# Scaling the last two output tiles of a two-branch gated layer in halves, on ScalarE and VectorE

## The chip, the cores and the metric

The kernel runs on one core of a Trainium2 chip. The metric is device time in microseconds (us) of one execution; lower is better. The engines are TensorE (PE in the profile, with its weight loads as PEld), VectorE (DVE), ScalarE (ACT), GpSimd (POOL) and SyncE (SP); PSUM is the memory into which TensorE writes.

## The reference

Two branches work on the same input `x` of 2048 rows and 512 columns, and a gate of each row mixes them:

```
g = sigmoid((x * gate_w).sum(-1))
a = state-space branch: a complex linear recurrence over the 2048 rows, then
    2 * Re(h @ C^T) + x * Dskip
b = linear attention with 32 heads of 16 columns: features of q and k by softmax,
    num / (den + 1e-6), then @ wo
out = g * a + (1 - g) * b          (2048 x 512, bfloat16)
```

The input `B_x` is given but not used: both branches read `A_x`.

## The kernel before, in words

The 2048 rows are cut into 16 tiles of 128 rows. A tile of the output (a "row" in the rest of this text, numbered `n` from 0 to 15 in the order in which it is made) goes through three small generators, and each `yield` in them ends a step:

- `y{n}` (`st_y`, lines 709 to 723) begins the output of the row in a PSUM tile `py` of 128 partitions x 512 fp32 columns, which fills one PSUM bank. Its matmuls add the state-space branch (L717) and `x * Dskip` (L722).
- `o{n}` (`st_o`, lines 725 to 759) makes the attention branch of the row. Matmuls put the numerators and denominators into `pn` (L736); ScalarE takes the logarithm of the denominators, ScalarE or VectorE copies the numerators to `nu`, ScalarE makes `rd`, which holds the reciprocal denominators and also `(1 - g) / g`, and VectorE multiplies both into `on` (L744). For rows 12 to 15 (`OT_PE`) TensorE transposes `on` into a PSUM tile `po` (L753), and a copy brings it to `oT` in SBUF (`evac`, L119 on ScalarE or L121 on VectorE). For the other rows a transposing DMA does this (L758).
- `t{n}` (`st_t`, lines 761 to 774) ends the row. First step: four matmuls of `oT` with `Wo` add into `py` (L765). Second step: one instruction scales `py` by the gate of each row, `G[:, ti:ti + 1]`, and writes the bfloat16 tile `ot` (L769 on ScalarE, L771 on VectorE). Third step: one DMA of 128 KB writes `ot` to the output (L773).

No planner orders the work. A list written out by hand, `ORDER`, names the steps one by one, and the loop at the end of the kernel calls `next` on the named generator; every engine then executes its instructions in this order. A suffix `:D` on a step makes it use VectorE instead of ScalarE for its copy or scaling, `:A` sends its DMA from ScalarE's queue instead of SyncE's, and `@k` names the PSUM bank. The framework adds the waits between engines (semaphores) by itself, from the tiles that the instructions read and write. The list ends with:

```
... y13 t13 o14 o14@1 t15 t15 t15 o14:D t14 t13 t13 t14 t14:A
```

Read step by step: row 13's output matmuls; the product `on` of row 14; its transposes on TensorE; row 15's output matmuls, its scaling on ScalarE, its DMA from SyncE; the copy of row 14's `po` to `oT` on VectorE (`o14:D`); row 14's output matmuls; row 13's scaling and DMA; row 14's scaling on ScalarE and its DMA from ScalarE's queue. So row 15 ends before row 14, and row 14 is the last of all.

Of the kernel before, what the change touches and what calls it, by code (L numbers as in the profile page):

```python
# [10 lines left out]
ALU = mybir.AluOpType  # L11
# [57 lines left out]
def kernel(  # L69
# [18 lines left out]
    nc = tc.nc  # L88
    _, S, D = A_x.shape
# [5 lines left out]
    NTI = S // P  # L95
# [12 lines left out]
    VS = nc.vector.tensor_scalar  # L108
# [3 lines left out]
    sel = {"banks": [], "eng": "act"}  # L112
# [66 lines left out]
    G = const.tile([P, NTI], F32, name="G")  # L179
# [581 lines left out]
    def st_t(n):  # L761
        ti = order[n]
        py, oT = live["py", n], live["oT", n]
        for g in range(HG):
            MM(out=py[:], lhsT=oT[:, g, :], rhs=Wo[:, g, :], start=False, stop=(g == HG - 1))  # L765
        yield
        ot = pools["op"][1].tile([P, D], BF16, name="ot", bufs=14)
        if sel["eng"] == "act":
            nc.scalar.mul(out=ot[:], in_=py[:], mul=G[:, ti:ti + 1])  # L769
        else:  # L770
            VS(out=ot[:], in0=py[:], scalar1=G[:, ti:ti + 1], scalar2=None, op0=ALU.mult)  # L771
        yield
        sel["q"].dma_start(out=out_par[:, ti // 2, ti % 2, :], in_=ot[:])  # L773
        yield
# [17 lines left out]
    for n in range(NTI):  # L792
        st.update({f"k{n}": st_k(n), f"v{n}": st_v(n), f"q{n}": st_q(n), f"y{n}": st_y(n), f"o{n}": st_o(n), f"t{n}": st_t(n)})
# [10 lines left out]
    for tok in ORDER.split():  # L804
        tok, _, eng = tok.partition(":")
# [42 lines left out]
```

## Time and profile before

| | us |
|---|---|
| median of 3 timed runs | 155.96 (155.78 to 157.13) |
| time of the profiled execution | 155.28 |
| span of the profiled execution, first to last instruction | 153.2 |

| engine | busy us | share of the span |
|---|---|---|
| PE | 146.2 | 95% |
| DVE | 132.4 | 86% |
| ACT | 129.2 | 84% |
| POOL | 15.8 | 10% |

The profile is of one execution, and its time of 155.28 us lies 2.1 us above its span, which holds only what lies between the first and the last instruction. In a timeline row the columns are: start (us from the span's start), length (us), engine, source line, operation, output<-input, number of instructions merged into the row, and in brackets how long the engine had been idle and what ended it. A row with `q` behind the engine (`SPq`, `ACTq`) is of the engine's instruction sequencer, such as the issue of a DMA. In a group row the number before the bar is the count, then come the total busy time, the mean ns of one instruction, and the idle time ahead of them.

### The profile page before, as it was taken

The page shows a single profiled execution, that of the slowest core. Times are in us where ns is not written, and L with a number is a line of the kernel's source. Part 1 is how long each engine was busy: PE and PEld are TensorE (multiplying, and loading weights), DVE is VectorE, ACT ScalarE, POOL GpSimd, SP SyncE. Part 2 cuts the span into 40 slices and gives each one's busy share as a digit, 9 for nine tenths or more (in the row PEclk, how much of TensorE's full clock was granted, in tenths as well). Part 3 has the DMA queues.
Part 4 walks back from the last instruction along what each step waited for, and adds up shares of the span by engine and source line. Part 5 has one row for each costly group of instructions (what it writes and reads, how often), then busy time and mean ns, then how long its engine had stood idle before and what let it go on. Part 6 is the DMA issues. An engine that isn't in the chain of part 4 may idle for free.

```text
span 153.2 us, 3361 instructions
## 1 busy us (share of the span) xinstructions
PE 146.2 (95%) x1236; PEld 95.0 (62%) x1254; DVE 132.4 (86%) x303; ACT 129.2 (84%) x279; POOL 15.8 (10%) x43
## 2 busy tenths in 40 slices
PE   7899999999999999999999999999999999999990
PEld 7644434788878985869867656555554455555540
DVE  3799999999999999999999999999999958717520
ACT  3489998999998999999998999699498998627562
POOL 8239980000000000000000000000000000000000
PEclk9999999999999999999999999999999999999997
DMA  4875995534445699930000007711278859969842
GB/s 116 164 218 97 223 178 112 103 75 103 103 107 78 129 230 178 166 115 4 0 0 4 0 0 169 74 37 34 42 98 147 176 122 189 162 129 206 247 143 103
DMA packets 50848, 17.55 MB, mean 115 GB/s; under 512 B 44176, under 2 KB 50832, under 8 KB 50832
## 3 DMA queue, kind: packets, MB, share of 16 engines
q1 hardware_dynamic: 48976, 15.75, 53.8%
q10 hardware_dynamic: 1696, 1.57, 3.2%
q8 instruction: 10, 0.16, 0.5%
q0 software_dynamic: 160, 0.01, 0.2%
q14 instruction: 6, 0.05, 0.1%
HBM read 2.64 MB, written 2.10 MB: 31 GB/s over the span
## 4 chain that ended last, share of the span: by engine, by line
PE 78%; SPq 10%; DMA 7%; issue 1%; ACT 1%
PE pgq L601 18%; PE py L717 16%; PE pq L475 9%; PE py L765 8%; SPq L229 8%; PE pv L475 4%; PE ph L668 4%; PE pk L475 4%; DMA xT<-in_A_x_dram 4%; PE kvacc L578 3%; DMA phT<-EEq 3%; PE pn L736 3%; PE pgq L606 2%; PE py L722 2%; PE pgq L608 2%; SPq L284 1%
## 5 line engine op out<-in xcount | busy, mean ns | idle before, releaser
L601 PE MATMUL pgq<-xT,BT 128*128 128x256 bf16 x256 | 31.5, 272 | 0.0
L475 PEld LDWEIGHTS <-xT 128*128 128x128 bf16 x192 | 18.2, 98 | 18.3 <-DMA xT<-in_A_x_dram 0.7
L601 PEld LDWEIGHTS <-BT 128*128 128x128 bf16 x256 | 24.6, 98 | 4.1
L138 ACT ACTIVATE EEk<-EEk 128x1024 bf16<-128x1024 bf16 x20 | 20.4, 1080 | 0.0
L119 ACT CAST uv<-pgq 128x512 bf16<-128x512 f32 x28 | 15.9, 605 | 0.5 <-PE pgq L601 0.4
L475 PE MATMUL pv<-Wv,xT 128*128 128x512 bf16 x59 | 15.5, 379 | 0.3
L475 PE MATMUL pq<-Wq,xT 128*128 128x512 bf16 x60 | 15.4, 379 | 0.2
L765 PE MATMUL py<-Wo,oT 128*128 128x512 bf16 x62 | 15.3, 379 | 0.1
L475 PE MATMUL pk<-Wk,xT 128*128 128x512 bf16 x62 | 14.7, 379 | 0.3 <-DMA xT<-in_A_x_dram 0.2
L138 ACT ACTIVATE EEq<-EEq 128x1024 bf16<-128x1024 bf16 x12 | 11.7, 1042 | 0.3 <-DVE EEq L527 0.3
L769 ACT ACTIVATE ot<-py,G 128x512 bf16<-128x512 f32 x12 | 7.9, 686 | 4.5 <-PE py L765 4.3
L138 ACT ACTIVATE ld<-pn 128x16 f32<-128x16 f32 x32 | 6.1, 191 | 5.7 <-PE pn L736 4.6
L590 ACT ACTIVATE phT<-X,dgB 128x512 bf16<-128x512 bf16 x16 | 10.7, 725 | 0.0
L119 ACT CAST nu<-pn 128x256 bf16<-128x256 f32 x27 | 9.9, 380 | 0.0
L119 ACT CAST vx<-pv 128x512 bf16<-128x512 f32 x16 | 9.1, 604 | 0.4 <-PE pv L475 0.4
L548 DVE TENSOR_TENSOR EEk<-EEk,rck 128x4096 bf16<-128x4096 bf16 (+1 forms) x5 | 9.3, 1858 | 0.0
L744 DVE TENSOR_TENSOR on<-nu,rd 128x512 bf16<-128x512 bf16 x16 | 6.7, 421 | 2.8 <-ACT rd L138 1.6
L765 PEld LDWEIGHTS <-oT 128*128 128x128 bf16 x64 | 5.7, 97 | 5.3 <-DMA oT<-on 0.5
L119 ACT CAST Xq<-pq 128x512 bf16<-128x512 f32 x16 | 8.9, 608 | 0.0
L119 ACT CAST Xq<-pk 128x512 bf16<-128x512 f32 x15 | 8.6, 598 | 0.4 <-PE pk L475 0.4
L736 PEld LDWEIGHTS <-phT 128*128 128x128 bf16 x128 | 6.2, 97 | 3.8 <-DMA phT<-EEq 1.4
L511 DVE TENSOR_TENSOR smk<-smk 128x512 bf16<-128x512 bf16 (+4 forms) x18 | 8.1, 448 | 0.1
(178 smaller groups left out, 321.2 us busy)
## 6 DMA issues: line engine op xcount, KB each, us to landing
X<-HM SPq DMA_DIRECT2D x8, 256.0 KB, 4.5
out_dram<-ot ACTq DMA_DIRECT2D x8, 128.0 KB, 2.5
out_dram<-ot SPq DMA_DIRECT2D x8, 128.0 KB, 2.2
C2r<-in_B_wqkv_dram ACTq DMA_DIRECT2D x2, 256.0 KB, 3.8
Wv<-in_B_wqkv_dram SPq DMA_DIRECT2D x1, 512.0 KB, 4.0
Bn<-in_A_B_re_dram SPq DMA_DIRECT2D x1, 512.0 KB, 5.7
Bn<-in_A_B_im_dram SPq DMA_DIRECT2D x1, 512.0 KB, 6.8
Wo<-in_B_wo_dram SPq DMA_DIRECT2D x1, 512.0 KB, 4.3
```

The costliest lines, as they stand in the source:

```text
L119: nc.scalar.copy(out=out_ap, in_=in_ap)
L138: ins = nc.scalar.activation(**kw)
L229: nc.sync.dma_start_transpose(out=xT[:, :, ti * P:(ti + 1) * P], in_=x_res[ti // 2, ti % 2])
L475: MM(out=pt[:], lhsT=xT[:, kt, ti * P:(ti + 1) * P], rhs=W[:, kt, :], start=(kt == 0), stop=(kt == KT - 1))
L511: VT(out=dst, in0=cur[:, :, :, 0:n, :], in1=cur[:, :, :, n:2 * n, :], op=op)
L548: VT(out=E5, in0=E5, in1=rc.to_broadcast([P, L, 2 * NB, Dh, 4]), op=ALU.mult)
L590: nc.scalar.mul(out=t_, in_=x_, mul=c_)
L601: MM(out=pg[:, h, :], lhsT=BT[:, kt, 2 * j + h, :], rhs=xT[:, kt, r * NC:(r + 1) * NC], start=(h == 0 and kt == 0), stop=(r % 2 == 0 and k ...
L717: MM(out=py[:], lhsT=hs(r, t, slice(a * P, (a + 1) * P)), rhs=C2B[t], start=(t == 0), stop=False)
L736: MM(out=pn[:, 4 * m:4 * m + 4, :].rearrange("p h e -> p (h e)"), lhsT=ph[:, 4 * hf + m, :], rhs=KVm[:, 4 * hf + m, :], start=(m == 0), st ...
L765: MM(out=py[:], lhsT=oT[:, g, :], rhs=Wo[:, g, :], start=False, stop=(g == HG - 1))
L769: nc.scalar.mul(out=ot[:], in_=py[:], mul=G[:, ti:ti + 1])
```

## The change

For the last two rows, `n` of 14 and 15, the single scaling instruction becomes two. ScalarE scales columns 0 to 255 and VectorE columns 256 to 511 of the same `py` tile into the same `ot` tile. The suffix of the step is not looked at for these two rows. The list `ORDER` is the same word for word, the DMAs are the same, and rows 0 to 13 are scaled as before. The lines below the edit move down by three: L769 becomes L772, L771 becomes L774, L773 becomes L776; the new halves are L769 (ScalarE) and L770 (VectorE).

```
         yield
         ot = pools["op"][1].tile([P, D], BF16, name="ot", bufs=14)
-        if sel["eng"] == "act":
+        if n >= NTI - 2:
+            nc.scalar.mul(out=ot[:, 0:D // 2], in_=py[:, 0:D // 2], mul=G[:, ti:ti + 1])
+            VS(out=ot[:, D // 2:D], in0=py[:, D // 2:D], scalar1=G[:, ti:ti + 1], scalar2=None, op0=ALU.mult)
+        elif sel["eng"] == "act":
             nc.scalar.mul(out=ot[:], in_=py[:], mul=G[:, ti:ti + 1])
         else:
             VS(out=ot[:], in0=py[:], scalar1=G[:, ti:ti + 1], scalar2=None, op0=ALU.mult)
```

## The prediction, made before the changed kernel was run

> **What bounds the kernel now.** I read the head of the page first, then the chain that ended last at its tail, then the timeline of that tail.
>
> ```profile
> span 153.2 us, 3361 instructions
> PE 146.2 (95%) x1236; PEld 95.0 (62%) x1254; DVE 132.4 (86%) x303; ACT 129.2 (84%) x279; POOL 15.8 (10%) x43
> PE 78%; SPq 10%; DMA 7%; issue 1%; ACT 1%
> ```
>
> TensorE sets the pace of the whole kernel: it is busy 95% of the span and carries 78% of the chain. The change touches nothing but the last two rows of the output, so the shares of the whole run are no help. What counts is the last 6 us, where TensorE has run out of work. There the chain reads (start, length, what):
>
> ```profile
> 147.44 0.88 PE py L765 x4
> 148.32 0.02 issue
> 148.34 0.89 ACT ot L769 x2
> 149.23 0.27 issue
> 149.50 0.69 ACT ot L769
> ```
>
> After row 15's four output matmuls, ScalarE's three scalings stand in a row (t15, t13, t14) and the end hangs on the third. The timeline, asked in narrow windows so that merged rows come apart, shows the other engines around it:
>
> ```profile
> 147.28 0.38 PE L765 MATMUL py<-Wo,oT 128*128 128x512 bf16 x1
> 147.48 0.42 DVE L121 COPY oT<-po 128x512 bf16<-128x512 bf16 x1 [1.06 <-PE po L753]
> 147.96 0.10 PEld L765 LDWEIGHTS <-oT 128*128 128x128 bf16 x1
> 148.14 1.03 PE L765 MATMUL py<-Wo,oT 128*128 128x512 bf16 x4
> 148.34 0.69 ACT L769 ACTIVATE ot<-py,G 128x512 bf16<-128x512 f32 x1 [1.00 <-PE py L765]
> 148.93 1.25 ACT L769 ACTIVATE ot<-py,G 128x512 bf16<-128x512 f32 x2
> 149.50 0.69 ACT L769 ACTIVATE ot<-py,G 128x512 bf16<-128x512 f32 x1
> 150.22 0.34 ACTq L773 DMA_DIRECT2D out_dram<-ot  x1
> DMA to landing us min/median/max: 2.0/2.0/2.0
> ```
>
> The last row here is the landing time of that one final transfer. The reader is to see a piece of luck in the order: VectorE copies row 14's transposed tile (`oT<-po`) at 147.48, while TensorE is still on row 15's matmuls (first at 147.28). Row 14's weights are loaded at 147.96, and its four matmuls follow without a gap (148.14 to 149.17). ScalarE takes t15 at 148.34, t13 at 148.93 and t14 at 149.50, ends at 150.19, and the transfer goes out at 150.22. It lands 2.0 us later, at 152.2. The span ends about 1.0 us after that (153.2), with the closing waits of the program, and the profiled time of 155.28 us lies 2.1 us above the span.
>
> **The change part by part.** Two scalings of 128x512 on ScalarE become halves of 128x256, and VectorE gets two halves of 128x256. Nothing goes to another queue and no transfer is added. What decides is where the new instructions stand, and for what they wait. The built order of the changed kernel has at its end, engine by engine (line, instruction, tile, what it waits for):
>
> ```
> DVE  L770 ot_2496<-py_2290 128x256 [waits Activation]   row 15
>      L121 oT_2486<-po_2487 128x512                      row 14
>      L770 ot_2508<-py_2264 128x256 [waits Activation]   row 14
> ACT  L769 ot_2496<-py_2290 128x256 [waits PE]           row 15
>      L772 ot_2505<-py_2046 128x512                      row 13
>      L769 ot_2508<-py_2264 128x256 [waits PE]           row 14
>      L776 out<-ot_2508 [waits DVE]                      row 14
> SP   L776 out<-ot_2496 [waits DVE]                      row 15
> ```
>
> Two things follow. First, the halves do not run at once: each VectorE half waits for ScalarE's counter to count the ScalarE half of the same row, so a row's scaling takes the one half after the other. Second, the copy `oT<-po` of row 14 now stands on VectorE behind the row 15 half. It used to start at 147.48, and it must now wait for row 15's matmuls, for ScalarE's half and for VectorE's half. Behind that copy waits TensorE, with row 14's four matmuls, and behind those the end of the kernel.
>
> The prices of a half are not in the trace. The nearest groups are (mean ns of one after the bar):
>
> ```profile
> L769 ACT ACTIVATE ot<-py,G 128x512 bf16<-128x512 f32 x12 | 7.9, 686 | 4.5 <-PE py L765 4.3
> L119 ACT CAST uv<-pgq 128x512 bf16<-128x512 f32 x28 | 15.9, 605 | 0.5 <-PE pgq L601 0.4
> L119 ACT CAST nu<-pn 128x256 bf16<-128x256 f32 x27 | 9.9, 380 | 0.0
> L771 DVE TENSOR_SCALAR ot<-py,G 128x512 bf16<-128x512 f32 x4 | 3.0, 750 | 4.2 <-PE py L765 4.1
> L121 DVE CAST Wk<-pf 128x512 bf16<-128x512 f32 x2 | 1.4, 686 | 0.0
> L121 DVE CAST nu<-pn 128x256 bf16<-128x256 f32 x5 | 2.0, 423 | 2.6 <-ACT ld L138 2.6
> ```
>
> On ScalarE half the columns of a cast take 605 - 380 = 225 ns off; so a half scaling costs 686 - 225 = 461 ns, not 343. On VectorE they take off 686 - 423 = 263 ns; a half costs 750 - 263 = 487 ns, not 375. Bounds: halving the whole (343 and 375) from below, the whole itself (686 and 750) from above. I take the differences, since they come from the same engines on casts of these very sizes. So a row's two halves in turn cost about 0.46 + 0.49 = 0.95 us and a handover, where one scaling cost 0.69.
>
> The Trainium skill, "ScalarE: Activation LUTs", section "What ACT_TABLE_LOAD costs", gives an activation with a per-row operand as about 280 ns and 0.833 ns for each column: 707 ns for 512, where the trace has 686, and 493 ns for 256. With 493 ns for both ScalarE halves the sum below would be 0.06 us more.
>
> Handovers come from these rows:
>
> ```profile
> 140.03 0.18 ACT L138 ACTIVATE ld<-pn 128x16 f32<-128x16 f32 x1
> 140.25 0.42 DVE L121 CAST nu<-pn 128x256 bf16<-128x256 f32 x1 [0.26 <-ACT ld L138]
> 144.74 0.75 DVE L771 TENSOR_SCALAR ot<-py,G 128x512 bf16<-128x512 f32 x1
> 145.40 0.41 DVE L121 COPY oT<-po 128x512 bf16<-128x512 bf16 x1
> 22.88 0.11 PEld L475 LDWEIGHTS <-xT 128*128 128x128 bf16 x2 [0.65 <-DMA xT<-in_A_x_dram]
> 22.89 0.39 PE L475 MATMUL pk<-Wk,xT 128*128 128x512 bf16 x1 [0.16 <-DMA xT<-in_A_x_dram]
> ```
>
> ScalarE to VectorE takes 0.04 (140.21 to 140.25). A copy behind a scaling on VectorE starts 0.09 before the scaling's end (145.49, 145.40). VectorE's copy to the weight load takes 0.06 (147.90 to 147.96), and a waiting TensorE starts its first matmul 0.01 after the weight load (22.88, 22.89). The matmuls' end to ScalarE takes 0.03 (148.31, which is 147.28 and 1.03, to 148.34), and the last scaling's end to the issue of its transfer 0.03 (150.19 to 150.22).
>
> The sum, from 148.34, which the change leaves where it is:
> - row 15 on ScalarE 148.34 to 148.80; on VectorE 148.84 to 149.33
> - copy of row 14's tile 149.24 to 149.66 (0.42), where it ran 147.48 to 147.90
> - weight load 149.72, matmuls 149.73 to 150.76 (1.03), where they ended at 149.17
> - row 14 on ScalarE 150.79 to 151.25; on VectorE 151.29 to 151.78
> - transfer issued at 151.81 instead of 150.22: **+1.59 us**
>
> What lies beside this: row 13's scaling, on ScalarE from about 148.70 (0.10 ahead of the end before it, as at 148.93 against 149.03) to 149.38, is hidden in the wait for VectorE, so the 0.23 us gained there is lost. Row 15's transfer starts some 0.3 us later than before and row 13's behind it on SP's queue, both more than 1.5 us ahead of the last one, so they cost nothing; if that cover were gone, they would land at about 152, still ahead of 153.8. The last transfer still takes 2.0 us.
>
> So the profiled execution goes from 155.28 to 156.87 us. The three timed runs have a median of 155.96 (155.78 to 157.13), 0.68 above it; the forecast is the median and the difference, **157.55 us**.
>
> **The rivals.** (a) The halves do run at once, as the change's words have it, with the copy still behind the row 15 half. VectorE's half then runs 148.34 to 148.83, the copy 148.74 to 149.16, matmuls 149.23 to 150.26, both last halves until 150.78, issue 150.81: +0.59, 156.55 us. For it speaks that the trace shows ScalarE and VectorE busy together all along; against it stands the wait in the built order. The Trainium skill, "PSUM — Partial Sum Buffer", section "PSUM bank collisions raise a hardware error", says that software must keep two engines off the same bank and quadrant of partitions at any one time, for two reads as well. No run here shows what happens otherwise. By it the two halves of one row, which lie in one bank, could not be read together at all.
>
> (b) Not slower: the copy of row 14 gets through before row 15's half, because its input has been ready since about 147.46. Row 14's matmuls then end at 149.17 as before, ScalarE has its half at 149.28 to 149.74, VectorE its own until 150.27, issue 150.30: +0.08; with the halves at once, issue 149.77: -0.45, 155.51 us. It decides whether the copy starts before 148.34. Against it: VectorE's order puts the copy after the half, and rows 144.74 and 145.40 show a scaling and such a copy run one behind the other, in order.
>
> (c) TensorE now stands idle for 1.42 us (148.31 to 149.73), and if its clock were halved by then, the last four matmuls would take 2.06 instead of 1.03: +2.62, 158.58 us. What the trace has on it are windows after TensorE's last matmul (the granted clock is the number after the last bracket):
>
> ```profile
> 151.00:151.50 0.50, 0.00 (x0) 0.00 (x0) 0.00 (x0) 0.00 (x0) 0.00 (x0) 1.00 0.73 258
> 151.50:152.00 0.50, 0.00 (x0) 0.00 (x0) 0.00 (x0) 0.00 (x0) 0.00 (x0) 0.67 0.02 4
> 152.00:152.50 0.50, 0.00 (x0) 0.00 (x0) 0.00 (x0) 0.00 (x0) 0.00 (x0) 0.50 0.00 0
> ```
>
> The clock is still full at 151.50 and halves within the next slice, more than 2.3 us after the end at 149.17. An idle stretch of 1.42 us is shorter, so this is unlikely.
>
> **How the numbers follow.** My forecast, halves in turn with the copy behind them, has 0.84; (a) 0.07, (b) 0.04, (c) 0.05. A difference of 1% is 1.56 us, about what a measurement of this kernel can tell from no change, and my sum of 1.59 lies just above it. With halves at their lower bounds the sum would be 1.59 - 2 x (0.118 + 0.112) = 1.13, and at the upper ones 1.59 + 2 x (0.225 + 0.263) = 2.57. The handovers are taken at the tightest rows there are, so they lean upward. Of the 0.84 I put 0.55 over 1% and 0.29 within. Slower by over 1%: 0.55 and (c), 0.60. Within 1%: 0.29, (a) and half of (b), 0.38. Faster by over 1%: 0.02, the other half of (b), were more gained than its price. The forecast's own range is 157.1 to 158.5, by its bounds; the range given reaches down to (a), 156.5, and up to 158.5.
>
> **What would show it.** In the changed kernel's timeline: VectorE's first half starts right after ScalarE's half has ended, not with it; the copy `oT<-po` starts near 149.2; TensorE has a gap of about 1.4 us ahead of its last four matmuls, which still take 1.03; the last transfer is issued near 151.8; halves take about 0.46 and 0.49. It would be wrong if both halves started together, if TensorE had no gap there, or if the tail stood as before and the time differed elsewhere.

## The result, and the profile after

Over 18 runs each, the changed kernel takes 157.32 us (156.38 to 157.99) and the kernel before 155.49 us (154.82 to 157.23); the 18 of before include the three runs of the table above. The ratio is 1.0105, with a 95% interval of 1.0082 to 1.0129: the change makes the kernel 1% slower. The forecast was 157.55 us, 1.0102 times the median of before, in a range of 156.5 to 158.5. Executions come in a faster and a slower state, and all ratios and medians here are of the fast ones.

The head of the page of the changed kernel hides all this. TensorE's busy share is what it was, and the one trace of the change in the chain is that VectorE now has 1% of it (TensorE's 75% of the chain against 78% is none: a second profile of the kernel before has 82%):

```profile
span 155.7 us, 3362 instructions
PE 147.3 (95%) x1236; PEld 96.1 (62%) x1254; DVE 133.2 (86%) x305; ACT 128.9 (83%) x279; POOL 15.8 (10%) x43
PE 75%; SPq 10%; DMA 10%; issue 1%; DVE 1%; ACT 1%
```

The end of that chain (start, length, what) has become longer:

```profile
149.37 0.02 issue
149.39 0.48 ACT ot L769
149.87 0.02 issue
149.90 0.48 DVE ot L770
150.38 0.34 DVE oT L121
150.72 0.05 issue
150.77 1.05 PE py L765 x4
151.82 0.02 issue
151.84 0.48 ACT ot L769
152.32 0.02 issue
152.35 0.48 DVE ot L770
```

Before, this chain went through three scalings on ScalarE and was done. Now it goes from ScalarE's half of row 15 to VectorE's half, from there to the copy of row 14's tile (`oT`, L121), to row 14's four matmuls, and once more through a ScalarE half and a VectorE half. The timeline of the changed kernel shows the same from the engines' side, with the waits in brackets:

```profile
149.39 0.47 ACT L769 ACTIVATE ot<-py,G 128x256 bf16<-128x256 f32 x1 [0.87 <-PE py L765]
149.76 0.68 ACT L772 ACTIVATE ot<-py,G 128x512 bf16<-128x512 f32 x1
149.90 0.48 DVE L770 TENSOR_SCALAR ot<-py,G 128x256 bf16<-128x256 f32 x1 [1.98 <-ACT ot L769]
150.30 0.41 DVE L121 COPY oT<-po 128x512 bf16<-128x512 bf16 x1
150.77 1.04 PE L765 MATMUL py<-Wo,oT 128*128 128x512 bf16 x4 [1.42 <-DVE oT L121]
151.84 0.47 ACT L769 ACTIVATE ot<-py,G 128x256 bf16<-128x256 f32 x1 [1.40 <-PE py L765]
152.35 0.48 DVE L770 TENSOR_SCALAR ot<-py,G 128x256 bf16<-128x256 f32 x1 [1.64 <-ACT ot L769]
152.87 0.34 ACTq L776 DMA_DIRECT2D out_dram<-ot  x1
DMA to landing us min/median/max: 1.9/1.9/1.9
```

VectorE's half waits for `ACT ot L769`, the other half of its own row, and TensorE waits 1.42 us for `DVE oT L121`, a copy whose input was long ready. I call the stretch from the start of row 15's scaling to the issue of the last transfer the tail (in the profile of before it is 1.88 us; the expectations below have 1.87). It is 149.39 to 152.87 here, 3.48 us, against 148.34 to 150.22, 1.88 us, before: **+1.60 us**. (In these two profiles row 15's scaling also starts 1.05 us later, 149.39 against 148.34. What that is worth is a question for the experiments.)

### The profile page after: what moved, and what is told of

Same layout as the page of the kernel before. It is cut to its first block, busy times and chain, and to the rows that moved or that the text cites. A ratio compares the mean times of both kernels' runs of the same rounds, so it can differ in the third digit from the quotient of the medians.

```text
span 155.7 us, 3362 instructions
## 1 busy us (share of the span) xinstructions
PE 147.3 (95%) x1236; PEld 96.1 (62%) x1254; DVE 133.2 (86%) x305; ACT 128.9 (83%) x279; POOL 15.8 (10%) x43
## 4 chain that ended last, share of the span: by engine, by line
PE 75%; SPq 10%; DMA 10%; issue 1%; DVE 1%; ACT 1%
PE pgq L601 18%; PE py L717 14%; PE pq L475 9%; PE py L765 8%; SPq L229 8%; PE pv L475 4%; PE ph L668 4%; PE pk L475 4%; DMA xT<-in_A_x_dram 4%; DMA oT<-on 3%; DMA phT<-EEq 3%; PE kvacc L578 3%; PE pn L736 2%; PE pgq L606 2%; PE py L722 2%; PE pgq L608 2%
## 5 line engine op out<-in xcount | busy, mean ns | idle before, releaser
L772 ACT ACTIVATE ot<-py,G 128x512 bf16<-128x512 f32 x10 | 6.8, 688 | 4.1 <-PE py L765 4.0
```

## The experiments

Theory A puts the loss down to the copy of row 14 that stands behind row 15's VectorE half; rival B to the halves that run in turn; rival C to a delay ahead of the tail.

**Copy first.** The halves stay, and the copy goes ahead of row 15's scaling:

```
 ORDER (on top of the changed kernel)
-o14@1 t15 t15 t15 o14:D t14 t13 t13 t14 t14:A
+o14@1 t15 o14:D t15 t15 t14 t13 t13 t14 t14:A
```

> Both rows in halves as in the changed kernel, but the copy of row 14's transposed tile stands ahead of row 15's scaling in the step list. The tail is counted from the start of row 15's scaling to the issue of the last transfer: 1.87 us in the kernel before, 3.48 in the changed one. Theory A (the loss is the copy that stands behind row 15's VectorE half): row 14's matmuls end as before, ScalarE has row 14's half from about 0.96 to 1.43 and VectorE its own from 1.47 to 1.95, tail 1.98, time +0.1 us, ratio 1.001 to the kernel before. Rival B (the loss is the halves that run one after the other, each row paying it): two rows at 0.3 us each, +0.6, ratio 1.004. Rival C (the change delays the work ahead of the tail: row 15's scaling started 1.05 us later in the profile after): that delay stays, tail near 2.0 but time +1.1, ratio 1.007.

Measured: a ratio of 1.0006 (0.9973 to 1.0039), a tail of 1.96 us. VectorE's timeline of this kernel, with ScalarE's two halves and the last transfer:

```profile
148.72 0.42 DVE L121 COPY oT<-po 128x512 bf16<-128x512 bf16 x1 [1.27 <-PE po L753]
149.59 0.47 ACT L769 ACTIVATE ot<-py,G 128x256 bf16<-128x256 f32 x1 [1.00 <-PE py L765]
150.09 0.48 DVE L770 TENSOR_SCALAR ot<-py,G 128x256 bf16<-128x256 f32 x1 [0.95 <-ACT ot L769]
150.53 0.47 ACT L769 ACTIVATE ot<-py,G 128x256 bf16<-128x256 f32 x1
151.03 0.48 DVE L770 TENSOR_SCALAR ot<-py,G 128x256 bf16<-128x256 f32 x1 [0.46 <-ACT ot L769]
151.55 0.34 ACTq L776 DMA_DIRECT2D out_dram<-ot  x1
```

The copy waits only for its own transposes. Both rows still run their halves in turn, and all but 0.08 us of the loss is gone. The halves in turn are not free even so: row 14's half starts 0.94 us into the tail, where its whole scaling started at 1.16 before, since ScalarE has only half of row 15 ahead of it, and that nearly pays for VectorE's half behind it. Rival B falls by the tail, where two rows at 0.3 us would have made about 2.5 us; by the time it would not, since 0.6 us is a ratio of 1.0038, still inside the interval. Rival C wanted 1.007, which lies outside.

**Row 15 alone, row 14 alone.** The condition `n >= NTI - 2` becomes `n == NTI - 1` in the one and `n == NTI - 2` in the other.

> Halves for row 15 alone, row 14 whole on ScalarE. Theory A: the copy still stands behind row 15's VectorE half, so only row 14's halves are saved: tail 3.48 - (0.47 + 0.03 + 0.48) + 0.69 = 3.18, +1.30 us, ratio 1.008. Rival B: row 15's halves cost 0.3 and the rest comes from elsewhere: tail 2.2, +0.3, ratio 1.002. Rival C: tail 3.18 and 1.0 more ahead of it, +2.3, ratio 1.015.

> Halves for row 14 alone, row 15 whole on ScalarE. Theory A: the copy is at its old place, and the last scaling takes 0.47 + 0.03 + 0.48 in turn where it took 0.69: tail 1.87 + 0.31 = 2.18, +0.3 us, ratio 1.002. Together with the kernel that has row 15 alone in halves (+1.30) this makes the whole 1.6. Rival B: about the same as row 15 alone. Rival C: +1.3, ratio 1.008. If the halves of one row could run at once, the tail would be 1.87 - 0.2 and the ratio below 1.

Measured: row 15 alone 1.0075 (1.0038 to 1.0111), tail 3.17 us; row 14 alone 0.9993 (0.9960 to 1.0025), tail 2.17 us. The two tails are 1.29 and 0.29 above 1.88, together 1.58 of the whole 1.60. Rival B had both rows at about 0.3: that is the price of row 14 and not of row 15. For row 14 alone the 0.29 us, a fifth of a per cent, is shown by the trace and lies within the interval of the times. In the timeline of row 15 alone, the copy is again behind the half, and row 14's whole scaling waits for the matmuls that wait for the copy:

```profile
150.34 0.47 ACT L769 ACTIVATE ot<-py,G 128x256 bf16<-128x256 f32 x1 [0.87 <-PE py L765]
150.85 0.48 DVE L770 TENSOR_SCALAR ot<-py,G 128x256 bf16<-128x256 f32 x1 [1.98 <-ACT ot L769]
151.25 0.41 DVE L121 COPY oT<-po 128x512 bf16<-128x512 bf16 x1
152.80 0.69 ACT L772 ACTIVATE ot<-py,G 128x512 bf16<-128x512 f32 x1 [1.40 <-PE py L765]
153.51 0.34 ACTq L776 DMA_DIRECT2D out_dram<-ot  x1
```

**No halves, the same queue.** If the queue is the cause, a whole scaling at that place must do harm too:

```
 ORDER (on top of the kernel before)
-o14@1 t15 t15 t15 o14:D t14 t13 t13 t14 t14:A
+o14@1 t15 t15:D t15 o14:D t14 t13 t13 t14 t14:A
```

> No halves: the kernel before with row 15's scaling, whole, on VectorE instead of ScalarE, at the same place of the list, so ahead of the copy of row 14's tile. Theory A (the price is the copy queued behind a scaling that waits for row 15's matmuls, whatever that scaling is): scaling 0 to 0.75, copy 0.67 to 1.08, matmuls 1.14 to 2.17, row 14 on ScalarE 2.21 to 2.90, issue 2.93: tail 2.93 us against 1.87, +1.06, ratio 1.007. Rival B (the price is the halves in turn): there are none here and ScalarE has one scaling less, so the tail is at most 1.87 and the ratio at most 1.000.

Measured: 1.0072 (1.0039 to 1.0106), tail 2.93 us. Not one scaling is split here, and two thirds of the loss are there:

```profile
149.67 0.75 DVE L771 TENSOR_SCALAR ot<-py,G 128x512 bf16<-128x512 f32 x1 [2.13 <-PE py L765]
150.34 0.41 DVE L121 COPY oT<-po 128x512 bf16<-128x512 bf16 x1
151.89 0.69 ACT L769 ACTIVATE ot<-py,G 128x512 bf16<-128x512 f32 x1 [2.06 <-PE py L765]
152.60 0.34 ACTq L773 DMA_DIRECT2D out_dram<-ot  x1
```

**Halves with a bank each.** Why do the halves wait for each other? In the next kernel columns 256 to 511 of rows 14 and 15 are accumulated in a PSUM tile `p2` of their own (`p` in the profile, which leaves numbers out), and the matmuls of these two rows become twice as many, of 256 columns each. The new step `u14` or `u15` in the list makes the matmuls of `p2` that `y14` or `y15` made earlier. The output tile `ot` stays one, shared by both halves, and the copy stays where the change had it:

```
+    def st_u(n):                      # columns 256 to 511 of row n, in another bank
+        p2 = bank([P, D // 2], F32, "p2")
+        ...                           # its 8 matmuls of L717 and 2 of L722
 ORDER (on top of the changed kernel)
-... o15 t10 o13:D t11 ... o14@1 t15 t15 t15 ...
+... o15 t10 o13:D u14@4 t11 ... o14@1 u15@2 t15 t15 t15 ...
```

> The changed kernel with columns 256 to 511 of rows 14 and 15 accumulated in PSUM tiles of their own (other banks), so that VectorE's half has nothing to do with ScalarE's; same work, matmuls of 256 columns there, and the copy still behind row 15's half. If the halves wait for each other because they share a PSUM tile, they now start together: row 15 0 to 0.48, copy 0.40 to 0.82, matmuls 0.87 to 1.91, halves 1.95 to 2.43, issue 2.46: tail 2.46 against 3.48 of the changed kernel and 1.87 before, +0.6, ratio 1.004. Rival (the two engines slow each other when they read PSUM at once): halves longer than 0.47 and 0.48, tail above 2.5.

Measured over six runs: 1.0215 (1.0161 to 1.0268), tail 2.62 us. The timeline at row 15 and at row 14:

```profile
151.92 0.47 ACT L786 ACTIVATE ot<-py,G 128x256 bf16<-128x256 f32 x1 [2.87 <-PE py L779]
152.03 0.48 DVE L787 TENSOR_SCALAR ot<-p,G 128x256 bf16<-128x256 f32 x1 [3.93 <-PE p L780]
153.88 0.47 ACT L786 ACTIVATE ot<-py,G 128x256 bf16<-128x256 f32 x1 [0.91 <-PE py L779]
153.98 0.48 DVE L787 TENSOR_SCALAR ot<-p,G 128x256 bf16<-128x256 f32 x1 [1.14 <-PE p L780]
154.54 0.34 ACTq L793 DMA_DIRECT2D out_dram<-ot  x1
```

VectorE's half now waits for its matmuls (`PE p`) and no longer for ScalarE, though both still write one `ot`. So it was the shared PSUM tile, and not the shared `ot`, that made the halves wait; whether the tile or its bank counts is not told apart, since both changed together. They overlap and are as long as before, 0.47 and 0.48, so the rival of a mutual slowdown falls. The tail is 0.16 above the 2.46 expected: ScalarE's half, from whose start it is counted, begins one matmul ahead (0.11), and the issue follows VectorE's end by 0.08 (153.98, 0.48 and then 154.54) instead of 0.03. The time, however, was expected at 1.004, and that is a miss by 1.7%, all but 0.16 us of it outside the tail. The Trainium skill, "PSUM — Partial Sum Buffer", section "Specifications (TRN2)", says that ScalarE and VectorE read PSUM in parallel at full bandwidth as long as they do not meet in a bank; these rows agree, with 0.47 and 0.48 us side by side as in turn.

**The best of it.** Row 14 alone in halves, with its own bank; row 13's scaling on VectorE behind the copy (`o14:D t14 t13:D t13 t14 t14:A`); row 15 whole on ScalarE. And row 13 on VectorE by itself, with no halves, which was timed twice.

> Row 14 alone in halves, with a bank of its own for VectorE's half, and row 13's scaling whole on VectorE behind the copy; row 15 whole on ScalarE. Theory A: copy at its old place, row 14's matmuls end 0.86 after row 15's, both halves 0.90 to 1.38, issue 1.41: tail 1.41, -0.46 us against before and -0.17 against row 13 on VectorE alone, ratio 0.997. Rival: the extra weight loads and matmuls of 256 columns cost TensorE more than that ahead of the tail: tail 1.41 but ratio 1.000 or above.

> No halves at all; the kernel before with row 13's scaling, whole, on VectorE behind the copy, where VectorE stands idle. Theory A, turned round (the end hangs on ScalarE's queue of three scalings): the last scaling no longer waits behind row 13's and starts 0.04 after row 14's matmuls, 0.29 earlier: tail 1.58, -0.29 us, ratio 0.998. Rival: the end is set by the transfers, and row 13's and row 14's now go out closer together, so nothing is gained: ratio 1.000.

> Row 13's scaling whole on VectorE and no halves, timed once more on another chip, since its first ratio, 0.9986, left open whether its 0.29 us shorter tail shows in the time. If it does: ratio 0.997 to 0.999 again and a tail of 1.58. If not: ratio around 1.000.

Measured: with the bank, tail 1.44 us and ratio 1.0062 (1.0033 to 1.0090); row 13 alone, tail 1.58 both times, ratios 0.9986 (0.9954 to 1.0019) and 0.9994 (0.9961 to 1.0028). So both tails are shorter than before, as reckoned; yet the one kernel is slower, and for the other the 0.3 us stay unproven in the time. The rival had the first come out so, but by more work for TensorE, and the busy time does not show that: it is 147.4 us there and 147.4 us in the second profile of the kernel before. What the traces show instead are TensorE's waits in the last third, from 100 us to the tail: first of the kernel before, then of row 14 with its own bank, then of both rows with theirs (sum, times, longest):

```profile
PE pn L736 <- DMA phT<-EEq: 0.2, 1, 0.2
...
PE py L782 <- DMA oT<-on: 0.7, 1, 0.7
PE pn L749 <- DMA phT<-EEq: 0.6, 2, 0.5
...
PE pn L749 <- DMA phT<-EEq: 1.8, 4, 1.1
PE py L782 <- DMA oT<-on: 0.8, 1, 0.8
```

These waits for transposing transfers are 1.3 and 2.6 us, and the time lost outside the tail in the table below is 1.3 and 2.5. It would fit that the matmuls which were put off had covered them; but this is not shown, for it is one profile of each, no run was made with the matmuls put off and nothing else, and kernels that put nothing off can have such waits too. The kernel with row 15 alone in halves has 1.7 us of them:

```profile
L765 PE MATMUL py<-Wo,oT 128*128 128x512 bf16 x64 | 16.1, 379 | 3.1 <-DMA oT<-on 1.7
```

What no other profile has is the wait for `phT`, 0.6 and 1.8 us here against 0.3 at most elsewhere. So the time lost is shown by the runs, and its cause only in part.

**Before and after once more.**

> The kernel before, unchanged, profiled once more. Rival C (the change delays the work ahead of the tail) needs row 15's scaling to start near 148.3 us here again. Theory A says that its start moves from execution to execution by more than 1 us whatever the kernel (so far 148.3 to 150.3 us in six kernels), with the tail at 1.87.

> The changed kernel as it is, timed and profiled once more beside the kernel before. Theory A: tail again 3.48 us (+1.60 against 1.87), ratio 1.009 to 1.011, and what lies ahead of the tail within 0.3 us of the kernel before, by the medians. Rival C: the part ahead of the tail is later by about 1 us here too, and the ratio stays near 1.017.

Measured: the kernel before has its tail at 148.90 to 150.78, 1.88 us; the changed one at 150.72 to 154.20, 3.48 us, and the ratio 1.0088 (1.0051 to 1.0125), not the 1.017 of rival C, which the first 1.0105 had not borne out either. The start of the tail differs by 0.56 us between two profiles of the one kernel and by 1.33 between two of the other. The table sets all kernels side by side; the rest is the median less the tail, and its difference is to the kernel before in the same comparison, whose tail is taken as 1.88.

| kernel | tail expected | tail | median us | before us | rest, against before |
|---|---|---|---|---|---|
| the change | 3.47 | 3.48 | 157.32 | 155.49 | +0.2 |
| the change again | 3.48 | 3.48 | 157.11 | 155.86 | -0.35 |
| copy first | 1.98 | 1.96 | 156.00 | 155.93 | 0.0 |
| row 15 alone | 3.18 | 3.17 | 157.34 | 155.93 | +0.1 |
| row 14 alone | 2.18 | 2.17 | 155.96 | 155.93 | -0.3 |
| row 15 whole on VectorE | 2.93 | 2.93 | 157.17 | 155.84 | +0.3 |
| row 13 on VectorE | 1.58 | 1.58 | 155.77 | 155.93 | +0.1 |
| row 13 on VectorE again | 1.58 | 1.58 | 155.98 | 155.86 | +0.4 |
| both rows, own banks | 2.46 | 2.62 | 159.11 | 155.84 | +2.5 |
| row 14, own bank | 1.41 | 1.44 | 156.70 | 155.84 | +1.3 |

Where only the tail was touched, the rest moves by at most 0.4 us, up and down; for the change itself it is +0.2 and -0.35, where within 0.3 was expected of the second. So the delay of 1.05 us ahead of the tail seen in the first profile after is no price of the change, and rival C falls at that size; a few tenths either way these times cannot tell.

What makes the start of the tail move is in part in the traces: from 100 us to the tail TensorE waited for transposing transfers 0.2 us and not at all in the two profiles of the kernel before, 0.7 and 1.6 us in the two of the changed kernel. That is 0.9 of the 1.33 us between these two. In all five profiles in which VectorE scales row 15 or half of it these waits are 0.7 to 1.7 us, and in the five others without a bank of their own 0.2 at most. The times of these kernels show no such difference, so whether it is chance stays open.

## Why the prediction was right

The step that carried it was to read, in the built order, what each new instruction waits for and what stands behind it. By its own terms, predicted and measured in the profile after:

| term | predicted | measured |
|---|---|---|
| ScalarE half | 0.461 | 0.473 |
| VectorE half | 0.487 | 0.484 |
| ScalarE to VectorE | 0.04 | 0.03 to 0.04 |
| idle TensorE ahead of row 14 | 1.42 | 1.42 |
| row 14's four matmuls | 1.03 | 1.04 |
| last transfer, from issue to landing | 2.0 | 1.9 |
| tail, against before | +1.59 | +1.60 |

The prices of a half are the rows of this group, asked over the whole of the changed kernel:

```profile
L770 DVE TENSOR_SCALAR ot<-py,G 128x256 bf16<-128x256 f32 x2 | 1.0, 484 | 3.6 <-ACT ot L769 3.6
L769 ACT ACTIVATE ot<-py,G 128x256 bf16<-128x256 f32 x2 | 0.9, 473 | 2.3 <-PE py L765 2.3
```

Taking them as the whole less the difference of two casts was good to 12 and 3 ns; halving the whole would have been 130 and 109 ns short, 0.48 us in the sum for four halves. The estimate of 493 ns that the prediction worked out from the Trainium skill ("ScalarE: Activation LUTs", section "What ACT_TABLE_LOAD costs") lies 20 ns above the 473 measured.

Of the rivals, (a), halves at once, does not take place: each VectorE half waits for its row's ScalarE half. Its price was of the right kind: with a bank each the halves do run together and the tail stands 0.74 above before, 0.15 more than the +0.59 given. (b), the copy ahead of the half, was made so in the experiment and cost 0.08, as priced (tail 1.96 against 1.88). (c), a halved clock, did not come: the matmuls took 1.04 us after an idle stretch of 1.42 us, and the granted clock of that stretch (the number after the last bracket) was full:

```profile
149.90:150.30 0.40, 0.00 (x0) 0.00 (x0) 0.40 (x2) 0.40 (x1) 0.00 (x0) 1.00 0.00 0
150.70:151.20 0.50, 0.43 (x2) 0.21 (x3) 0.01 (x1) 0.00 (x0) 0.00 (x0) 1.00 0.00 0
```

But the reason that the prediction gave against (c) does not hold. It had the clock stay full for more than 2.3 us after TensorE's last work, from the one profile of before. In the second profile of the changed kernel the last matmuls ran from 152.10 to 153.14, and the clock fell within 0.8 us of that:

```profile
152.10 1.04 PE L765 MATMUL py<-Wo,oT 128*128 128x512 bf16 x4 [1.42 <-DVE oT L121]
153.50:153.70 0.20, 0.00 (x0) 0.00 (x0) 0.01 (x1) 0.15 (x1) 0.00 (x0) 1.00 0.06 15
153.90:154.10 0.20, 0.00 (x0) 0.00 (x0) 0.20 (x1) 0.00 (x0) 0.00 (x0) 0.50 0.00 0
```

So the time since the last matmul does not decide it by itself. That row 14's matmuls ran at full clock is what the three profiles with a gap of 1.42 us ahead of them show (1.04 us each time); the argument that put (c) at 0.05 was too sure.

The mechanism and the size of the tail were right, and not by luck. One reading is loose: TensorE works until 149.17, so it is out of work for the last 4 us and not for 6; the sum does not use it. Which side of 1% the time falls on, 1.59 us against 1.56, was open, and is luck: the measured ratios, 1.0105 and 1.0088, lie on either side. The forecast time came as close as 0.23 us partly because two misses offset each other: its base, the median of three runs, was 0.47 us above the median of 18, and the difference of the medians was 1.83 us, 0.24 more than the sum (in the second comparison it was 1.25). The prediction also took 1% to be about the least that can be told from no change; 18 runs left an interval of a quarter of a per cent on either side.

## What to carry to other kernels

Before giving an engine a new instruction, look at what stands behind it in that engine's order: VectorE ran its instructions in the order of the list in every profile here, so a copy whose input was long ready cost 1.3 us, because a half scaling that had to wait stood ahead of it, and moving one step of the list took the tail from 3.48 to 1.96 us. Splitting one PSUM tile between two engines did not make them work at once here, since the second waited for the first; with a bank each they overlapped. And a shorter end is no gain by itself: with a bank of its own for row 14 the tail was 0.44 us shorter, and the kernel lost 1.3 us ahead of it. That the matmuls put off for it had been covering a wait is likely, and not shown.

## What the runs showed of the hardware

The end of the program repeats far better than its time. The 1.88, 1.58 and 3.48 us of a tail came out the same to 0.01 us in two profiles each, while the runs of the kernel before alone spread from 154.8 to 157.3 us, and the start of the tail lay anywhere from 148.3 to 150.7 us in kernels that do the same up to there. A change of 0.3 us at the end can be read from the trace, where a dozen runs leave an interval of 0.3%, or 0.5 us, on either side.

The granted clock outlasts TensorE's last matmul by no fixed time: it fell 2.5 us after it in the kernel before (last matmul to 149.17; full until 151.50 and 0.67 on the mean of the next 0.5 us, so halved at about 151.7), within 0.8 us in the second profile of the changed kernel, and 3.3 us after it with the copy first (matmuls to 150.41, full until 153.70, 0.50 from 153.90 on).
